# An earlier order of the first loads and 51 dummy products in a fused attention and FFN kernel

## The chip, the cores and the metric

The kernel runs on one core of one Trainium2 chip. The metric is the device time of one execution in microseconds, the median of several. A core has five engines that run side by side and meet only at semaphores: TensorE (PE) multiplies matrices, VectorE (DVE) and ScalarE (ACT) read its results and compute row by row, GpSimd (POOL) does small work in on-chip memory and issues some transfers, and SyncE (SP) issues the other transfers. Transfers are carried out by 16 DMA engines, which all queues share.

## The reference

For each of 8 batches with 12 heads, 448 positions and 64 values a head, the reference computes attention whose scores are mixed over the heads before the softmax and after it, and then a feed-forward network on all 3584 positions:

```python
scores = scale * np.matmul(q, k.transpose(0, 1, 3, 2))
scores = np.einsum('bhij,hg->bgij', scores, w_pre)
scores = scores - np.max(scores, axis=-1, keepdims=True)
attn = np.exp(scores)
attn = attn / (np.sum(attn, axis=-1, keepdims=True) + 1e-09)
attn = np.einsum('bhij,hg->bgij', attn, w_post)
attn_out = np.matmul(attn, v)
x = attn_out.transpose(0, 2, 1, 3).reshape(B * S, H * D)   # 3584 x 768
h = np.maximum(x @ w_in, 0.0)                              # 3584 x 2048
out = h * h @ w_out                                        # 3584 x 768
```

Inputs and output are float32; the kernel computes its products in bf16 with float32 sums.

## The kernel before, in words

**Stages of a batch.** q, k and v are loaded from HBM and cast to bf16 on the way, by transfers that POOL issues (`load_q`, `load_tail`, `load_kv`, lines 318 to 333). In the first two batches TensorE turns q and k with transposes (`t_qk` and `t_tail`, line 491 and line 519), and VectorE or ScalarE copies the results back. `score` (line 629) multiplies them: one product of 448 columns gives the scores of 128 positions of a head, which are cast from PSUM into `snat`. The scores must then be laid out anew, with positions and heads together along the partitions, so that the mixing over heads becomes a product: a transfer within on-chip memory that SP issues does this (`relayout`, `move`, line 658). In the following these transfers are called relayouts. Each of 45 chunks of a batch holds ten positions with their twelve heads. In the first 18 chunks of batch 0 a relayout of 315 KB serves three chunks, each mixed by three products (line 749, `wtri_all` with tiles lent by `osb` and `h2`); all other chunks have a relayout of their own of 105 KB and one product (line 753).

`chunk` carries a chunk through: the mixing product on TensorE; the row minimum on VectorE (line 758; signs are turned, so it stands for the maximum); the exponential with its row sum on ScalarE (line 761); the reciprocal on VectorE (line 767); the scaling of the second mixing matrix by it on GpSimd (line 770); four products that mix and transpose back (line 777); and a copy out of PSUM by VectorE or ScalarE (lines 395 and 397). When the chunks of a part are through, `av` multiplies by v (line 817). The FFN follows in units of 128 or 256 positions (`unit`): products with w_in (line 870), relu on ScalarE (line 883), the square on GpSimd (line 886), products with w_out (line 902), a copy on VectorE, and stores that SP issues. Units of FFN work have the lowest priority, so they fill TensorE's gaps; the first unit can begin only when the first parts of batch 0's attention are through.

**What sets the order.** All this work is first described as operations with an engine, a duration, a priority and dependencies. `Planner.run` plays it through before the program is built: at each moment each engine takes the ready operation with the lowest priority number, PSUM banks are given out, and two queues, LOAD and DMA, stand for the transfers. The order that comes out is the order in which each engine's instructions are written down. On the chip an engine keeps to that order, whatever arrives first. A chunk's priority is its number; its relayout has the number less `AHEAD` (line 43), which is the lead, in chunks, by which scores and relayouts go in front.

**The first batch.** Three transfers for k, two for the tails of q and three for q come first (`LOADS0`). The operation `started` stands for POOL's set-up and these eight issues. `first_batch` (line 1022) then waits for `opened`, a tiny copy on POOL of the first scores into `hold` (line 1036): only after it are v's two halves issued (`load_half`), and after them the six tiles of w_in (`load_w1`, line 988), each of 128 rows, 512 KB in bf16. The loads for batch 1 and the four parts of w_out (`load_w2`) follow at set chunks. `LAST_W1` (line 77) has no use in this version.

Of the kernel before, what the change touches and what calls it, by code (L numbers as in the profile page):

```python
# [39 lines left out]
PIECE = NPAIR // 2  # L40
NE = 6
NSCH = 11
AHEAD = 7.4
FIFO = 50
ROWS, COLS = 1, 2
TURN = 95
STAY = 2
# [26 lines left out]
TRI_IN = (0, 1)  # L74
W2_AT = [18, 21, 24, 27]
Q1_AT = [13, 16]
LAST_W1 = 4
TAIL0, Q0 = 19, 0.7
EARLY0 = 0

# [17 lines left out]
        self.last, self.wait = -1, -1  # L98


class Planner:

    def __init__(self):
        self.ops = []
        self.banks, self.most = [], {}

    def add(self, eng, ns, pri, fn, deps=(), lat=60, bank=None, frees=None, mode=0):
# [9 lines left out]
    def run(self):  # L119
# [22 lines left out]
        t, mode = 0, 0  # L142
        queues = {"LOAD": Queue(), "DMA": Queue()}

        def settle():
# [13 lines left out]
        while True:  # L159
            for eng, heap in ready.items():  # L160
                if eng in queues:
                    x = queues[eng]
                    y = queues["LOAD"]
                    if eng == "DMA" and x.op is None and heap and y.op is not None and x.last != t and x.wait < t:
                        ahead = max(0.0, y.left - (t - y.at) * y.rate) + sum(z[2].rows[0] for z in ready["LOAD"])
                        x.wait = t + int(min(ahead, FIFO) * y.op.rows[1])
                        heapq.heappush(events, (x.wait, n, None))
                        n += 1
                    if eng == "DMA" and x.wait > t:
                        continue  # L170
                    while x.op is None and heap:
                        op = heapq.heappop(heap)[2]
                        op.eng, op.at = eng, t
                        order.append((op, []))
                        if op.rows[0] == 0:
                            heapq.heappush(events, (t + op.lat, n, op))
                            n += 1
                            continue
                        x.op, x.left, x.at, x.rate = op, float(op.rows[0]), t, 0.0
                        settle()  # L180
                    continue
                if busy[eng] > t:
                    continue
                kept, short, first = [], False, None
                while heap:
                    item = heapq.heappop(heap)
                    op = item[2]
                    if op.eng is not None:
                        continue
                    wide = len(op.bank) > 1  # L190
                    if not fits(op) or (short and op.bank and op.bank[0][0] in HOLD):
                        short = short or wide
                        kept.append(item)
                        continue
# [12 lines left out]
                    args = []  # L207
                    break
                else:
                    item = None  # L210
                    if first is not None:
                        kept.remove(first)
                        item, op, args = first, first[2], []
                if item is not None:
# [21 lines left out]
            while events and events[0][0] == t:  # L236
# [21 lines left out]
                for x in op.next:  # L258
# [4 lines left out]
                        n += 1  # L263
                    elif x.left == 0:
                        push(x)
        assert len(order) == len(self.ops)
        return order


# [1 line left out]
def kernel(  # L271
# [57 lines left out]
    def load_kv(dst, src, b, h0, h1):  # L329
# [654 lines left out]
    w1_in, later = [], {}  # L984
    w2_in = [add("W2", 0, 0, lambda: None, lat=0) for i in range(4)]

    def load_w1(c2, pri, more=()):
        w1_in.append(load(16, (152, 148), pri, lambda: nc.gpsimd.dma_start(
            out=w1[c2][:, :], in_=moe_w_in[c2 * 128:(c2 + 1) * 128, 0:DFF], max_dma_last_dim=4096,
        ), [started, *more]))  # L990

    def load_w2(f4, n):
        f_, c_ = 8 * (f4 % 2), 384 * (f4 // 2)
# [3 lines left out]
        ), gate(n))  # L997
        done.next.append(w2_in[f4])
        w2_in[f4].left += 1

    def load_half(b, n, x, deps):
        h0 = x * H // 2
        v_in[b].append(load(42, (46, 58), n, lambda: load_kv(vs, v, b, h0, h0 + H // 2), deps))
# [17 lines left out]

    def first_batch():
        for i in range(NPAIR):
            if i == 0:
                v_in[0] = []
                for x in range(0):
                    load_half(0, -30 + x, x, [started])
        for p in range(NPAIR):
            t_qk(0, p)
        for g in range(2):  # L1030
# [1 line left out]
        for r in (1, 0):  # L1032
            for p in groups(0, r):
                score(0, r, p)
        hold = sb.tile([P, NPAIR], BF16, name="hold")
        opened = add("POOL", 150, -6, lambda: nc.gpsimd.tensor_copy(
            out=hold[:, :], in_=store_of(0, 0)[:, 0:NPAIR, 0],
        ), scopy[0, 0])
        for x in range(0, 2):
            load_half(0, -5 + 0.1 * x, x, [opened])  # L1040
        for i in range(NPAIR):
            load_w1(i, -4 + 0.1 * i, [opened])
        for n, c in enumerate(ORDER0):
            if c in C0[2:]:
                for p in groups(0, block_of(c)[0]):
# [50 lines left out]
    for b in range(B):  # L1096
# [4 lines left out]
        if b + 1 < B:  # L1101
# [4 lines left out]
                )  # L1106
            load_v(b + 1, (b + 1) * NCHUNK + 6, av_op[b, 0] + av_op[b, 1])

    guard = tc.manual_schedule(engines={
        mybir.EngineType.PE, mybir.EngineType.DVE, mybir.EngineType.Activation, mybir.EngineType.Pool, mybir.EngineType.SP,  # L1110
    })
# [33 lines left out]
```

## Time and profile before

| | |
|---|---|
| time, median of 3 runs | 590.29 us (589.7 to 591.21) |
| the profiled execution, its own time | 591.14 us |
| its span, first to last instruction | 589.4 us |
| TensorE busy | 565.2 us, 96% of the span, 5751 products |
| VectorE busy | 486.1 us, 82% |
| ScalarE busy | 471.3 us, 80% |
| GpSimd busy | 326.2 us, 55% |
| mean granted clock of TensorE | 0.99 |
| w_in's six transfers, 512 KB each | 21.8 us from issue to landing, median |
| v's transfers, 336 KB each | 9.6 us, median over all batches |

How to read it: the page cuts the span into 40 slices of 14.7 us and gives one digit for each, in tenths. TensorE's products are pipelined and their ends are modelled, so a busy TensorE is not TensorE at its peak; a single product's duration holds a fixed share besides its columns. The row PEclk is the clock granted to TensorE; 1.00 also stands where the profile has no record of a change yet. The rows of single instructions give start, duration, engine, line, operation, result and operands, and in brackets how long the engine had been idle before it and what ended that. `SPq` and the issues on POOL are the instructions that start transfers; how long the transfer itself takes is seen from who waits for it. In the rows of the DMA queues, q0 holds what GpSimd issues, here the loads, and q1 what SP issues, here relayouts and stores. Shares of DMA time above 1 occur, since packets of both queues are in flight together; they mean that the engines are full.

### The profile page before, as it was taken

What the parts mean: (1) busy time and instruction counts of PE and PEld (TensorE: products, weight loads), DVE (VectorE), ACT (ScalarE), POOL (GpSimd) and SP (SyncE); (2) the same over time, 40 slices, a digit from 0 to 9 for tenths busy, and PEclk for the clock granted to TensorE, in tenths of its full rate; (3) what the DMA queues carried; (4) which work ended last, traced back from release to release, by engine and by line L of the source; (5) the groups of instructions that cost most, each with busy time, mean ns of one, the idle gap of its engine ahead of it and who ended that gap; (6) DMA issues with size and microseconds to landing.
All of it is one profiled execution on the core that took longest, in us unless ns stands there. A gap on an engine that the chain in (4) does not pass through costs nothing.

```text
span 589.4 us, 17018 instructions
## 1 busy us (share of the span) xinstructions
PE 565.2 (96%) x5751; PEld 403.8 (69%) x5751; DVE 486.1 (82%) x1240; ACT 471.3 (80%) x1239; POOL 326.2 (55%) x600
## 2 busy tenths in 40 slices
PE   5698999999999999999999999999999999999996
PEld 3346766776668766776867776876767866867783
DVE  4697999997798998999898898989798898989201
ACT  4597998888988988989898878888889988788330
POOL 4436647546667437744865538744865624735340
PEclk9897999999999999999999999999999999999999
DMA  8899969984596449964596639974497547322021
GB/s 95 181 217 215 211 135 166 181 168 130 104 203 147 131 127 164 187 152 135 102 187 168 144 90 169 183 142 140 89 175 186 136 107 144 105 83 78 2 53 55
DMA packets 132086, 82.33 MB, mean 140 GB/s; under 512 B 59582, under 2 KB 126286, under 8 KB 131998
## 3 DMA queue, kind: packets, MB, share of 16 engines
q1 hardware_dynamic: 85214, 58.42, 40.6%
q0 software_dynamic: 46784, 22.81, 30.6%
q8 instruction: 45, 0.74, 0.5%
q14 instruction: 43, 0.35, 0.2%
HBM read 45.62 MB, written 11.01 MB: 96 GB/s over the span
## 4 chain that ended last, share of the span: by engine, by line
PE 84%; ACT 5%; DMA 5%; issue 2%; DVE 1%; SPq 1%; POOL 1%; DVEq 0%; POOLq 0%; ACTq 0%
PE bank L902 24%; PE bank L870 24%; PE bank L777 12%; PE bank L753 10%; PE bank L817 7%; PE bank L629 6%; DMA sch<-snat 3%; ACT es L761 2%; DMA osb<-snat 1%; SPq L658 1%; ACT snat L397 1%; ACT hr L883 1%; DVE mn L758 1%; PE bank L491 1%; DMA qt<-in_q_dram 1%
## 5 line engine op out<-in xcount | busy, mean ns | idle before, releaser
L761 ACT ACTIVATE es<-bank,mn 120x448 bf16<-120x448 f32 x360 | 229.4, 643 | 40.2 <-DVE mn L758 35.1
L770 POOL TENSOR_SCALAR wq<-wback,rc 120x120 bf16<-120x120 f32 x360 | 130.5, 367 | 179.4 <-DVE rc L767 104.2
L758 DVE TENSOR_REDUCE mn<-bank 120x1 f32<-120x448 f32 x360 | 209.5, 609 | 8.4 <-PE bank L749 5.2
L902 PE MATMUL bank<-w,h 128*128 128x384 bf16 x896 | 174.3, 325 | 0.9 <-ACT es L761 0.5
L395 DVE CAST atb<-bank 112x480 bf16<-112x480 f32 (+3 forms) x227 | 142.1, 634 | 30.8 <-PE bank L777 27.8
L870 PE MATMUL bank<-xt,w 128*128 128x256 bf16 (+1 forms) x1632 | 164.5, 254 | 0.2
L870 PEld LDWEIGHTS <-w 128*128 128x128 bf16 x1632 | 135.7, 98 | 21.9 <-issue 2.3
L886 POOL TENSOR_TENSOR h<-hr 128x512 bf16<-128x512 f32 x112 | 116.2, 1039 | 54.7 <-ACT hr L883 52.2
L777 PEld LDWEIGHTS <-es 120*112 120x112 bf16 (+1 forms) x1440 | 116.9, 130 | 39.5 <-issue 8.1
L777 PE MATMUL bank<-wq,es 120*112 120x120 bf16 (+1 forms) x1440 | 129.6, 218 | 2.8 <-POOL wq L770 1.9
L902 PEld LDWEIGHTS <-h 128*128 128x128 bf16 x896 | 83.5, 97 | 55.1 <-issue 5.6
L753 PE MATMUL bank<-sch,wmix 120*128 120x448 bf16 x334 | 103.9, 355 | 1.3 <-DMA sch<-snat 0.9
L395 DVE CAST snat<-bank 128x448 bf16<-128x448 f32 x164 | 96.0, 612 | 6.3 <-PE bank L629 3.5
L397 ACT CAST atb<-bank 112x480 bf16<-112x480 f32 (+3 forms) x157 | 82.3, 540 | 15.7 <-PE bank L777 14.2
L883 ACT ACTIVATE hr<-bank 128x512 f32<-128x512 f32 x112 | 67.1, 599 | 31.0 <-PE bank L870 25.2
L397 ACT CAST snat<-bank 128x448 bf16<-128x448 f32 x172 | 84.9, 550 | 4.3 <-PE bank L629 3.2
L761 ACT ACTIVATION_READ_ACCUMULATOR es<-bank,mn 120x1 f32 x360 | 75.7, 210 | 0.0
L767 DVE RECIPROCAL rc<-sm 120x1 f32<-120x1 f32 x360 | 52.7, 153 | 14.4 <-ACT es L761 12.3
L917 DVE COPY osb<-bank 128x384 f32<-128x384 f32 x56 | 30.7, 549 | 31.6 <-PE bank L902 31.3
L753 PEld LDWEIGHTS <-wmix 120*128 120x128 bf16 x342 | 30.3, 98 | 19.0 <-issue 7.8
L629 PE MATMUL bank<-kt,qz 64*128 64x448 bf16 x288 | 42.6, 354 | 0.5 <-ACT atb L397 0.2
L817 PE MATMUL bank<-atb,vs 112*64 112x192 bf16 (+3 forms) x864 | 42.2, 255 | 0.5 <-ACT atb L397 0.5
(57 smaller groups left out, 248.6 us busy)
## 6 DMA issues: line engine op xcount, KB each, us to landing
sch<-snat SPq DMA_DIRECT2D x318, 105.0 KB
out_dram<-osb SPq DMA_DIRECT2D x23, 360.0 KB
vs<-in_v_dram POOLq DMA_DIRECT2D x16, 336.0 KB, 9.6
ks<-in_k_dram POOLq DMA_DIRECT2D x14, 336.0 KB, 10.0
qs<-in_q_dram POOLq DMA_DIRECT2D x14, 288.0 KB, 8.2
w<-in_moe_w_in_dram POOLq DMA_DIRECT2D x6, 512.0 KB, 21.8
w<-in_moe_w_out_dram POOLq DMA_DIRECT2D x4, 768.0 KB, 24.5
out_dram<-osb SPq DMA_DIRECT2D x8, 192.0 KB
```

The lines of the kernel that those rows point to most:

```text
L395: nc.vector.tensor_copy(out=out_, in_=in_)
L397: nc.scalar.copy(out=out_, in_=in_)
L629: nc.tensor.matmul(slot[:, 0:S], lhsT=lhsT, rhs=kt[i][half, :, at_, :], start=True, stop=True)
L753: nc.tensor.matmul(slot[:, 0:S], lhsT=wm[0:rows, :], rhs=src[0:rows, :], start=True, stop=True,)
L758: nc.vector.tensor_reduce(out=mn[i][0:rows, :], in_=slots[mk][0:rows, 0:S], axis=AX.X, op=ALU.min)
L761: nc.scalar.activation(out=es[i][0:rows, 0:S], in_=slots[mk][0:rows, 0:S], func=ACT.Exp, scale=-1.0, bias=mn[i][0:rows, 0:1], accum_out=sm ...
L770: nc.gpsimd.tensor_scalar(out=wq[i][0:rows, :, 0:ns], in0=wback[0:rows, :, 0:ns], scalar1=rc[i][0:rows, 0:1], scalar2=1.0, op0=ALU.mult, o ...
L777: nc.tensor.matmul(slot[0:P_KEYS, jb * H * ns:(jb + 1) * H * ns], lhsT=es[i][0:rows, jb * P_KEYS:(jb + 1) * P_KEYS], rhs=wq[i][0:rows, :, ...
L817: nc.tensor.matmul(v_[64 * hh:64 * hh + 64, i, 0:x1 - x0], lhsT=vs[:, 2 * c2 + hh, jb, :], rhs=atb[half][:, jb, 2 * c2 + hh, x0:x1], start ...
L870: nc.tensor.matmul(slot[:, j * w:(j + 1) * w], lhsT=w1[c2][:, (f0 + j) * 128:(f0 + j + 1) * 128], rhs=xt[:, c2, a:z], start=(c2 == 0), sto ...
L886: nc.gpsimd.tensor_tensor(out=h2_[:, f0:f0 + nf, 0:w], in0=hr[gi % 2][:, :].rearrange("p (f c) -> p f c", f=nf), in1=hr[gi % 2][:, :].rear ...
L902: nc.tensor.matmul(slot[:, 0:384], lhsT=h2_[:, ft, mt * 128:(mt + 1) * 128], rhs=w2[:, ft, nt * 384:(nt + 1) * 384], start=(ft == 0), stop ...
```

## The change

It has three parts. First, the copy into `hold` and the wait for it go. The loads of the first batch depend on `started` alone and follow the q loads: one tile of w_in, then v's two halves, then the other five tiles.

Second, the planner gets a model of TensorE's clock and puts dummy products where it has TensorE idle. `Clock` divides time into spells of 3413 ns and keeps how much of each TensorE worked; below a share of `DROP` the plan's clock falls to half, from `RISE` on it returns, and TensorE's operations last twice as long in between. Before 130 us, if TensorE has nothing to do and a bank is free, and the clock is low or the last spell was worked for less than 0.55, a dummy is written down: a product of a tile of zeros, `still`, 256 columns wide, into the next free bank, which nobody reads. There are 51: 18 at the very start, before k arrives; 17 between the last scores of the second block and the first chunk's product; 3 among the products of chunks 20 to 22; and 13 among the first chunks of batch 1, ahead of the last attention products of batch 0. `still` is zeroed on VectorE as its first instruction.

Third, `AHEAD` goes from 7.4 to 7.2.

```diff
-AHEAD = 7.4
+AHEAD = 7.2
+IDLE_NS, IDLE_COLS, IDLE_FROM, IDLE_END, IDLE_LOW = 112, 256, 1300, 130000, 0.55
+SPELL, PHASE, DROP, RISE = 3413, 1700, 0.4, 0.8
-LAST_W1 = 4
+LAST_W1 = 1
+class Clock:
+    def __init__(self):
+        self.slow, self.edge, self.spells = True, PHASE, []
+
+    def at(self, t):
+        while t >= self.edge:
+            share = self.share(self.edge - SPELL, self.edge)
+            self.slow = share < (RISE if self.slow else DROP)
+            self.edge += SPELL
+        return 2 if self.slow else 1
+
+    def share(self, a, b):
+        return sum(max(0, min(b, z) - max(a, y)) for y, z in self.spells[-400:]) / (b - a)
...
+                if item is None and eng == "PE" and free and IDLE_FROM <= t < IDLE_END and (
+                    clock.at(t) > 1 or clock.share(t - SPELL, t) < IDLE_LOW
+                ):
+                    op = Op({"PE": 0}, 0, 0, self.still, [], None, None, mode)
+                    op.eng, op.ns, op.at = "PE", IDLE_NS * clock.at(t), t
+                    clock.spells.append((t, t + op.ns))
+                    order.append((op, [free[0], mode]))
...
-                        op.ns += TURN * (op.mode != mode)
+                        op.ns = (op.ns + TURN * (op.mode != mode)) * clock.at(t)
+                        clock.spells.append((t, t + op.ns))
...
+    still = sb.tile([P, IDLE_COLS], BF16, name="still")
+    nc.vector.memset(still[:, :], 0.0)
...
         for i in range(NPAIR):
-            if i == 0:
-                v_in[0] = []
-                for x in range(0):
-                    load_half(0, -30 + x, x, [started])
+            if i == LAST_W1:
+                load_v(0, 0.1 + i, [started])
+            load_w1(i, 0.1 + i)
...
-        hold = sb.tile([P, NPAIR], BF16, name="hold")
-        opened = add("POOL", 150, -6, lambda: nc.gpsimd.tensor_copy(
-            out=hold[:, :], in_=store_of(0, 0)[:, 0:NPAIR, 0],
-        ), scopy[0, 0])
-        for x in range(0, 2):
-            load_half(0, -5 + 0.1 * x, x, [opened])
-        for i in range(NPAIR):
-            load_w1(i, -4 + 0.1 * i, [opened])
...
+    def stand(slot, mode):
+        k_, m_ = P // 2 if mode == ROWS else P, P // 2 if mode == COLS else P
+        nc.tensor.matmul(
+            slot[0:m_, 0:IDLE_COLS], lhsT=still[0:k_, 0:m_], rhs=still[0:k_, :], start=True, stop=True,
+        )
```

More of the change, by code (lines that the diff above doesn't have):

```diff
@@ L107, in __init__ @@
         self.banks, self.most = [], {}
+        self.still = None
     def add(self, eng, ns, pri, fn, deps=(), lat=60, bank=None, frees=None, mode=0):
@@ L140, in fits @@
             return len(free) >= size and room[kind] >= size and (room["mix"] >= size or kind == "f")
-        t, mode = 0, 0
+        t, mode, clock = 0, 0, Clock()
         queues = {"LOAD": Queue(), "DMA": Queue()}
@@ L213, in run @@
                         item, op, args = first, first[2], []
+                if item is None and eng == "PE" and free and IDLE_FROM <= t < IDLE_END and (
[5 more added lines that the diff above has]
+                    order.append((op, [free[0], mode]))
+                    busy[eng] = t + op.ns
+                    heapq.heappush(events, (t + op.ns, n, None))
+                    n += 1
                 if item is not None:
@@ L265, in run @@
                         push(x)
-        assert len(order) == len(self.ops)
+        assert len(order) >= len(self.ops)
         return order
@@ L985, with load_w1 @@
     w2_in = [add("W2", 0, 0, lambda: None, lat=0) for i in range(4)]
-    def load_w1(c2, pri, more=()):
+    def load_w1(c2, pri):
         w1_in.append(load(16, (152, 148), pri, lambda: nc.gpsimd.dma_start(
             out=w1[c2][:, :], in_=moe_w_in[c2 * 128:(c2 + 1) * 128, 0:DFF], max_dma_last_dim=4096,
-        ), [started, *more]))
+        ), [started]))
     def load_w2(f4, n):
@@ L999, in load_w2 @@
         w2_in[f4].left += 1
-    def load_half(b, n, x, deps):
-        h0 = x * H // 2
-        v_in[b].append(load(42, (46, 58), n, lambda: load_kv(vs, v, b, h0, h0 + H // 2), deps))
     def load_v(b, n, deps):
@@ L1107 @@
             load_v(b + 1, (b + 1) * NCHUNK + 6, av_op[b, 0] + av_op[b, 1])
+    add("FIRST", 0, 0, lambda: None, lat=IDLE_FROM)
+    def stand(slot, mode):
[3 more added lines that the diff above has]
+        )
+    pl.still = stand
     guard = tc.manual_schedule(engines={
```

## The prediction

> **What bounds the kernel now.** I read the page's slices first, then the time by stretches of the front, then the order of time on TensorE, SP and POOL, then the two DMA queues by stretches.
>
> ```profile
> PE   5698999999999999999999999999999999999996
> PEclk9897999999999999999999999999999999999999
> ```
>
> Past slice 6 TensorE is full at full clock to the end, and from 55 us on its waits sum to 2.9 us (1.2 for GpSimd's scalings, the rest in halves and less). Time lost before some 57 us is thus lost for good; a gain there is kept as long as TensorE stays fed. The change acts in that front. By stretches (TensorE, weight loads, VectorE, ScalarE, GpSimd, granted clock, DMA share, GB/s):
>
> ```profile
> 15.00:20.00 5.00, 2.81 (x28) 1.08 (x25) 3.61 (x10) 3.71 (x9) 4.49 (x7) 1.00 0.52 92
> 20.00:24.30 4.30, 1.43 (x8) 0.52 (x6) 1.99 (x5) 1.95 (x6) 2.31 (x5) 1.00 1.11 188
> 24.30:28.00 3.70, 3.67 (x15) 1.93 (x16) 2.01 (x4) 1.38 (x4) 0.36 (x1) 0.54 1.15 272
> 28.00:45.00 17.00, 15.65 (x113) 7.66 (x112) 16.79 (x42) 15.92 (x41) 5.51 (x13) 1.00 1.07 221
> 45.00:51.30 6.30, 4.06 (x26) 2.11 (x24) 6.30 (x18) 5.21 (x14) 6.01 (x12) 0.77 1.27 208
> 51.30:57.00 5.70, 5.67 (x114) 4.97 (x115) 2.34 (x8) 3.58 (x13) 2.00 (x4) 0.66 1.40 220
> ```
>
> From 28 to 51.3 us VectorE (and nearly ScalarE) is the bound: a wait of another engine costs nothing there. VectorE's holes lie at 15 to 28 and at 51.3 to 57 us, and the granted clock is down in both. Who makes the first hole (SP issues the relayouts; x9 are three chunk products):
>
> ```profile
> 15.15 1.82 SPq L658 DMA_DIRECT2D osb<-snat  x2
> 19.56 1.86 PE L749 MATMUL bank<-osb,wtri_all 120*128 120x448 bf16 x9 [2.15 <-DMA osb<-snat]
> 24.33 2.31 PE L749 MATMUL bank<-osb,wtri_all 120*128 120x448 bf16 x6 [2.91 <-DMA osb<-snat]
> ```
>
> The first relayout lands 4.4 us after its issue, the second 8.3 us. Why, the DMA queues tell (q0 carries the loads, q1 the relayouts: packets, MB, share), for 12 to 18, 18 to 24, 24 to 31 and 31 to 39 us:
>
> ```profile
> q1 hardware_dynamic: 102, 0.27, 19.1%
> q0 software_dynamic: 31, 0.01, 1.7%
> ...
> q0 software_dynamic: 987, 0.51, 73.7%
> q1 hardware_dynamic: 196, 0.41, 23.0%
> ...
> q0 software_dynamic: 673, 0.76, 62.4%
> q1 hardware_dynamic: 503, 1.09, 51.5%
> ...
> q0 software_dynamic: 777, 1.50, 99.4%
> q1 hardware_dynamic: 169, 0.29, 11.4%
> ```
>
> The loads stand still for six microseconds (12 to 18). Then v, in many small packets, pushes the relayouts to 0.41/6 = 0.07 MB/us; beside w_in they get 1.09/7 = 0.16; alone they had 0.19 (in the second from 17). w_in alone gets 1.50/8 = 0.19.
>
> **The loads' new order.** The hold copy goes (POOL, 0.19 us). Eight issues (six of w_in at 0.72 us, two of v at 0.80, together 5.9) move from 15.7 to 8.4 us on POOL, which waits 6.9 us there (the hold's idle row). They end by 14.4, ahead of POOL's first softmax scaling at 22.35, so nobody waits for POOL. They pass nothing on SP. In q0 they follow the q loads, which drain by 11.7. The first w_in tile (0.51 MB at 0.19) runs to 14.4. v (0.69 MB, at 0.63/4 = 0.16 as k and q had from 8 to 12 us) has 0.37 MB through by 16.7, when the first relayout's packets start; the other 0.32, at v's shared 0.51/6 = 0.085, last to 20.5. Relayout 1 (0.32 MB) gets 0.26 by then and the rest at 0.16: it lands at 20.9 instead of 19.56. Relayout 2 then has w_in beside it instead of v: 0.32/0.16 = 2.0, so 23.0 instead of 24.33.
>
> (a) Chunk 3's products begin 1.3 us earlier. At full clock three products take 0.62 instead of the 1.15 of the row at 24.33, so VectorE, 0.77 behind the product's start as now for chunk 0 (19.56 to 20.33), has chunk 3 at about 23.8 instead of 25.56: -1.8. The first three chunks come 1.3 later, into a hole, and end before 23.8. TensorE then works through from 20.9, so the clock drop at 24.48 may not come: nine products at 558 ns instead of 353 are 1.85 of TensorE, inside VectorE's hole of 1.69. I count 0.3 of that, since the idle ahead of 20.9 may still pull the clock down. Sum -2.1; ends -3.5 (the hole of 24.3 to 28 gone too) and +2.0 (rival S).
>
> (b) w_in ends some 5 us earlier than the 47.4 of its last tile (issued 20.8, landing 26.6 later): q0 has used the idle six. TensorE's waits for relayouts at 45 to 51.3 us (about 2.9 with those of its weight loads) shrink, but VectorE is 6.30 of 6.30 busy over them, which is the cover. Batch 1's q and k, behind w_in in q0, land earlier also. -0.3; ends -2.9 (VectorE's order gives way too) and 0.3 (schedule against it).
>
> **The dummies.** One has 256 columns; at full clock twelve such products take 1.31 us, 109 ns each. Cold ones cost double: a chunk product takes 558 against 353, and the 205 more are its 448 columns at 0.43 ns (109/256) once again.
>
> (c) The first 18 last 18 x 0.218 = 3.9 us. The new memset on VectorE (0.13 to 0.38; the row of 384 words took 0.38) stands ahead of it: 1.2 to 5.1 us, inside TensorE's wait of 5.4 us for k. Their effect:
>
> ```profile
> L491 PE MATMUL bank<-ident,qs x12: 313/314/316, 12.7 to 13.2; 128*64 128x128 bf16 x12
> L491 PE MATMUL bank<-ident,qs x12: 219/219/243, 14.3 to 14.6; 128*64 128x128 bf16 x12
> ```
>
> TensorE was cold until some 14.2 us though the profile calls it 1.00, and the chain of waits from 7.75 to 14.7 is TensorE throughout. Warm, the streaming halves, but VectorE and ScalarE are 4.06 and 3.66 of 5 busy from 10 to 15 us, and relayout 1 waits for their casts: at most 0.9 earlier. Half of that: -0.4; ends -0.9, 0.
>
> A rule speaks against this part. The Trainium skill (TensorE: Matmul & The Clock Gate, Part 4: PE-mode transpose) says that transposes do not count as TensorE work the way products do, so full clock does not engage for them. The trace agrees so far: TensorE was busy without a gap from 8 us, mostly with transposes, and still cold six microseconds later. By that rule the warmth of the dummies is lost again before the scores.
>
> (d) 17 dummies (1.9 us) stand before the first chunk product, where TensorE idles 2.15 us now and 3.5 by (a): 0. Three stand near the products of chunks 20 and 21 (0.33, under VectorE's bound). Thirteen stand among batch 1's first products and the last attention products of batch 0 (1.42), where TensorE now has holes of 0.62, 0.60 and 0.47 (86 to 90 us). A dummy also waits for the last reader of the bank that the plan took for free, but the next product of that bank would wait for the same. Hidden: 0; the sixteen all on the path: 1.8. I take +0.5, nearer to the hidden end, since the holes of 1.69 lie where the thirteen stand.
>
> (e) The clock falls at 48.37 and 24.48 and rises at 27.89 and 55.19, all apart by multiples of 3.41 us. The second spell stretches 48 attention products to 2.77 us; the same 48 take 1.53 at 72.92. With the products around them it costs up to 2.0 of VectorE's 3.36 idle. The clock's steps may fall elsewhere in the next execution, since 3.41 us is their spacing and the profile of one execution gives one phase. Three dummies ahead and fewer waits for relayouts keep the clock up in perhaps two of five runs: -0.8; ends -2.0, 0.
>
> (f) Lead 7.2 instead of 7.4, with dummies and loads in the plan, reorders the engines from chunk 6 on; SP's first 57 instructions keep their order. No stage shows a price; bounds are TensorE's 3 us of waits past 55 us, either way. I take 0, and half of it for the range.
>
> Sum: -2.1 - 0.3 - 0.4 + 0.5 - 0.8 = -3.1 against the profiled execution (591.14, of it 589.4 span; the 1.7 around it stay). Its median of runs is 590.29, 0.85 lower, so 587.2.
>
> **Rivals.**
> - T, warmth lost: the rule above, (c) gives 0: 587.6. For it: cold until 14.2. Against: of the 6.6 us from 7.75 on, 2.95 are scores (0.56, 0.55, 0.93 and 0.91 by the rows), which do count.
> - N, front gain not kept: relayout 1's +1.3 cancels 2's -1.3, and both spells come back. VectorE's bound from 28 us covers the rest: -0.3 - 0.4 + 0.5 = -0.2, 590.1. For it: three dummies are few against 6.8 us of spell.
> - S, slower: relayout 1 meets w_in and v in full flow and flies 8.3 us like relayout 2 does now, landing at 23.45. The 1.99 us of VectorE from 20 to 24.3 move behind that, the spells stay: +2.0 - 0.3 + 0.5 = +2.2, 592.5. It decides from a landing of some 22.5 on. For it: v's 0.07 MB/us. Against: by 16.7 half of v should be through.
> - G: all good ends, -3.5 - 0.3 - 0.9 + 0.5 - 2.0 = -6.2: 584.1.
>
> **How the numbers follow.** This forecast 0.28, T 0.20, N 0.25, S 0.17, G 0.10. 0.3% is 1.8 us, about what a measurement here tells from no change: faster is below 588.5, slower above 592.1. With (f)'s 1.5 around each case: faster 0.24 + 0.16 + 0.10 + 0.03 = 0.53; slower 0.16 + 0.08 = 0.24; the rest 0.23. The range takes G's end and S with a little: 584.2 to 593.0; the forecast's own is 585.7 to 588.7.
>
> **What would show it.** The first chunk product's wait for its relayout ending at 20 to 21.5 us, and the next at 22.5 to 23.5, almost without idle between; a granted clock of 1.00 from 24.3 to 28; q0 moving from 12 to 18 us; w_in's last tile down by 43; transposes at 219 ns before 14 us (T: at 300 or more). Wrong if the first product comes after 22.5 (S), or the clock is 0.5 twice again (N).

## The result, and the profile after

The changed kernel takes 594.81 us (median of 6 runs, 593.39 to 597.26), the kernel before 590.79 (6 runs, 589.7 to 592.12): a ratio of 1.007, with a 95% interval of 1.0046 to 1.0094. It is some 4 us slower. The forecast was 587.2, and its range ended at 593.0. The profiled execution took 593.39, with a span of 591.6.

The slices of the changed kernel, TensorE and its granted clock:

```profile
PE   7787999999999999989999999999999999999996
PEclk8798999999999999999999999999999999999999
```

TensorE is as full as before past the front, but for a digit of 8 in the 18th slice (250 to 265 us), where before had a 9. By the same stretches as before (TensorE, weight loads, VectorE, ScalarE, GpSimd, granted clock, DMA share, GB/s):

```profile
15.00:20.00 5.00, 3.02 (x25) 1.81 (x22) 2.57 (x7) 2.68 (x7) 0.00 (x0) 0.98 1.28 210
20.00:24.30 4.30, 2.39 (x7) 0.99 (x7) 0.62 (x1) 0.42 (x1) 0.00 (x0) 0.50 1.10 272
24.30:28.00 3.70, 3.70 (x21) 1.82 (x19) 2.79 (x8) 2.51 (x9) 1.07 (x3) 0.69 1.10 274
28.00:45.00 17.00, 14.71 (x109) 7.24 (x108) 16.91 (x40) 15.46 (x39) 5.66 (x14) 1.00 0.59 134
45.00:51.30 6.30, 4.41 (x35) 2.48 (x34) 6.30 (x18) 6.23 (x20) 5.79 (x11) 1.00 1.19 155
51.30:57.00 5.70, 4.56 (x102) 3.81 (x102) 3.24 (x10) 3.21 (x11) 2.34 (x5) 0.73 1.35 231
```

From 20 to 24.3 us VectorE works 0.62 us, before it was 1.99; from 24.3 to 28 it works 2.79 instead of 2.01. VectorE's hole now lies earlier and has not shrunk, and both cold spells are there again: the clock is at 0.50 from 19.8 to 26.6 us, twice as long as in the kernel before (24.5 to 27.9), and from 53.9 to 57.3, half as long (48.4 to 55.2). The order of time in the front (start, duration, what; `L780` is the first chunks' product, `L689` the issue of a relayout, `L1131` the dummies), first of PE and then of SP:

```profile
1.06 4.02 PE L1131 MATMUL bank<-still 128*128 128x256 bf16 x18 [1.06 <-DVE still L365]
...
16.04 2.03 PE L1131 MATMUL bank<-still 64*128 64x256 bf16 x17
21.91 2.40 PE L780 MATMUL bank<-osb,wtri_all 120*128 120x448 bf16 x6 [3.85 <-DMA osb<-snat]
```

```profile
14.12 2.12 SPq L689 DMA_DIRECT2D osb<-snat  x2
```

Relayout 1 is issued 1.03 us earlier than before and lands 2.35 us later, at 21.9: a flight of 7.8 us, from the issue to the first product, where it was 4.4. The products behind it run at half clock, so that the next chunks follow 1.12 us apart. VectorE starts on the row minimum of chunk 3 one microsecond later than before (first line before, second line changed):

```profile
25.56 0.62 DVE L758 TENSOR_REDUCE mn<-bank 120x1 f32<-120x448 f32 x1 [3.04 <-PE bank L749]
```

```profile
26.58 0.62 DVE L789 TENSOR_REDUCE mn<-bank 120x1 f32<-120x448 f32 x1 [0.37 <-PE bank L780]
```

Why the flight is longer, the queues tell. From 14 to 18 us the loads' queue q0 has the first of these lines and q1 has none; in the microsecond from 18 to 19 the first packets of relayouts appear (second line); 18 to 24 us are the last two. The first share is above 100% with next to nothing in another queue, so packets of a single queue overlap too:

```profile
q0 software_dynamic: 1368, 0.76, 138.4%
...
q1 hardware_dynamic: 17, 0.05, 12.8%
...
q0 software_dynamic: 446, 0.81, 73.3%
q1 hardware_dynamic: 321, 0.76, 36.1%
```

At 18 us, 3.9 us after its issue, relayout 1 had not moved a byte, while the loads moved 0.76 MB from 14 us on; its first packets come between 18.5 and 19, so 4.4 to 4.9 us after the issue. Then both queues share, 0.13 MB/us each, and TensorE goes from relayout 1 to relayout 2 without a wait. In the kernel before, the first packets came 1.4 to 1.9 us after the issue (15.15, and 28 packets from 16.5 to 17).

### The profile page after: what moved, and what is told of

The parts are those of the page before. It is cut to its first block, busy times and chain, and to the rows that moved or that the text cites. A ratio compares the mean times of both kernels' runs of the same rounds, so it can differ in the third digit from the quotient of the medians.

```text
span 591.6 us, 17109 instructions
## 1 busy us (share of the span) xinstructions
PE 568.5 (96%) x5802; PEld 406.3 (69%) x5802; DVE 485.9 (82%) x1241; ACT 472.6 (80%) x1240; POOL 325.1 (55%) x598
## 4 chain that ended last, share of the span: by engine, by line
PE 81%; DMA 8%; DVE 6%; issue 2%; ACT 2%; SPq 1%; POOL 0%; DVEq 0%; POOLq 0%; ACTq 0%
PE bank L933 24%; PE bank L901 22%; PE bank L808 12%; PE bank L784 10%; PE bank L848 6%; PE bank L660 6%; DMA sch<-snat 4%; DVE mn L789 2%; DMA kt<-kn 2%; DVE atb L426 1%; DMA osb<-snat 1%; DVE snat L426 1%; PE bank L780 1%; ACT es L792 1%; DMA qt<-in_q_dram 1%
## 5 line engine op out<-in xcount | busy, mean ns | idle before, releaser
L426 DVE CAST atb<-bank 112x480 bf16<-112x480 f32 (+3 forms) x233 | 144.1, 631 | 31.1 <-PE bank L808 29.5
L808 PEld LDWEIGHTS <-es 120*112 120x112 bf16 (+1 forms) x1440 | 112.7, 130 | 38.7 <-issue 10.5
L808 PE MATMUL bank<-wq,es 120*112 120x120 bf16 (+1 forms) x1440 | 124.9, 217 | 5.5 <-POOL wq L801 4.6
L784 PE MATMUL bank<-sch,wmix 120*128 120x448 bf16 x334 | 102.7, 353 | 2.7 <-DMA sch<-snat 2.1
L428 ACT CAST atb<-bank 112x480 bf16<-112x480 f32 (+3 forms) x151 | 79.7, 540 | 13.6 <-PE bank L808 12.4
```

Of the source, the lines that this page charges most:

```text
L426: nc.vector.tensor_copy(out=out_, in_=in_)
L428: nc.scalar.copy(out=out_, in_=in_)
L784: nc.tensor.matmul(slot[:, 0:S], lhsT=wm[0:rows, :], rhs=src[0:rows, :], start=True, stop=True,)
L808: nc.tensor.matmul(slot[0:P_KEYS, jb * H * ns:(jb + 1) * H * ns], lhsT=es[i][0:rows, jb * P_KEYS:(jb + 1) * P_KEYS], rhs=wq[i][0:rows, :, ...
```

## The experiments

Each ratio below is against runs of the kernel before on the same chip, with its 95% interval. The new parts are called by three names: the order (lead and plan), the early loads, and the dummies. Where the order of the kernel before is kept, loads and dummies were moved or added in the finished order, so nothing else changes place. Two kernels were measured twice, and each pair came out 0.0017 or so apart, 1 us; differences of that size are at the edge of what can be told.

**The order, without early loads, with and without the dummies.** `e1_gated` keeps the changed kernel's order and its 51 dummies, but lets v and w_in wait for the hold copy again; `e6_order` is the same without the dummies.

```diff
+order = [x for x in order if x[0].fn is not stand]      # e6_order only
+at = 1 + max(i for i, x in enumerate(rest) if any(x[0] is y for y in scopy[0, 0]))
+order = rest[:at] + [(opened, [])] + [(x, []) for x in first_] + rest[at:]   # v0 v1 w0 .. w5
```

> The changed kernel with its order on every engine kept, dummies and lead 7.2 too; only the eight first loads go back behind the hold copy, in the old sequence (v's halves, then six tiles of w_in). Theory L (the early v loads hold relayout 1 back, and that is the loss): relayout 1 lands about 18.5 us instead of 21.9, the clock drop at 19.8 goes, and the time is 589 to 591.5, like the kernel before. Theory O (the new order past the front, from the lead and the new plan, is the loss): relayout 1 is early all the same, but the time stays at 593 to 595. Theory D (the 51 dummies stand in the way): 592 to 594.

> The changed kernel's order on every engine with the first loads back behind the hold copy and no dummies at all: the kernel before in all but the order. Theory O: 594.5 to 596 (2 above the same with its 51 dummies, since the front ones are worth about 2). If the order costs nothing: 591 to 592.

Measured: `e1_gated` 593.56 us, 1.0034 (1.0011 to 1.0057); `e6_order` 594.28 us, 1.006 (1.0028 to 1.0092). Both are near what theory O had, and relayout 1 lands at 18.3 in `e1_gated`, as forecast. The order alone costs 0.6%, 3.5 us, nearly as much as the whole change, and without its dummies the changed order is not shorter, which speaks against theory D. Where it loses, the stretches from 84 to 90 us and 84 to 132 us tell. The kernel before:

```profile
84.00:90.00 6.00, 4.27 (x58) 3.05 (x57) 5.51 (x16) 5.97 (x17) 3.47 (x7) 1.00 0.46 116
84.00:132.00 48.00, 46.27 (x520) 32.62 (x518) 45.24 (x118) 41.41 (x114) 28.23 (x56) 1.00 0.90 166
```

`e6_order`, the changed order alone:

```profile
84.00:90.00 6.00, 3.31 (x26) 2.17 (x24) 6.00 (x17) 4.55 (x14) 2.48 (x6) 0.83 0.53 149
84.00:132.00 48.00, 44.49 (x470) 30.80 (x469) 43.54 (x113) 38.49 (x106) 27.74 (x56) 0.93 0.85 160
```

Here batch 0 ends and batch 1 begins. In the plan before, VectorE and ScalarE share this work almost evenly (5.51 and 5.97 of 6); in the new one VectorE is full and ScalarE has 1.45 us free, and TensorE behind them loses 0.96 us. The chain there runs through GpSimd: TensorE waits for the scaling of the second mixing matrix, and GpSimd for a reciprocal that stands in VectorE's full order (`e6_order`):

```profile
85.88 0.37 PE L809 MATMUL bank<-wq,es 120*112 120x120 bf16 x4 [1.65 <-POOL wq L802]
```

```profile
87.74 0.37 POOL L802 TENSOR_SCALAR wq<-wback,rc 120x120 bf16<-120x120 f32 x1 [1.32 <-DVE rc L799]
```

In the kernel before the longest such wait of TensorE from 84 to 90 us is 0.62. In `e6_order` the clock also drops (0.93 over 48 us is 6.8 us at half speed). Over these 48 us TensorE makes 470 products instead of 520. The changed kernel itself:

```profile
84.00:90.00 6.00, 4.20 (x48) 3.18 (x46) 6.00 (x17) 4.73 (x14) 2.82 (x7) 1.00 0.59 167
84.00:132.00 48.00, 45.52 (x514) 31.72 (x512) 45.06 (x117) 40.31 (x111) 28.39 (x58) 1.00 0.87 171
```

The same full VectorE, but the clock stays up. Seven of the 22 more products from 84 to 90 us are dummies, and `e1_gated`, which has them too, also stays at 1.00. A second place is common to all kernels of this order, at 254 to 257 us, where before TensorE had no idle at all from 250 to 300 us. The chain of waits of the changed kernel, and TensorE's waits there:

```profile
246.61 9.12 DMA kt<-kn
```

```profile
PE bank L660 <- DVE atb L426: 0.9, 1, 0.9
PE bank L660 <- DMA kt<-kn: 0.7, 1, 0.7
```

VectorE's copies of the next k (`kn`) stand in its order ahead of copies that TensorE needs, and wait 1.85 us for the transfer that still reads the old `kn`. TensorE idles 1.62 us from 250 to 300 us in the changed kernel, 1.40 in `e1_gated`, 1.96 in `e6_order`.

**Is it the shorter lead, or any new plan?** `e4_lead`, `e15_lead73` and `e16_lead76` are the kernel before with only its lead changed to 7.2, 7.3 and 7.6 and planned anew. `e9_lead74` is the changed kernel, planned with a lead of 7.4.

```diff
-AHEAD = 7.4
+AHEAD = 7.2      # e4_lead; 7.3 in e15_lead73, 7.6 in e16_lead76
```

> The kernel before with the lead 7.2 instead of 7.4 and nothing else, so that the planner orders the work anew. Theory O: 592 to 595, and a stall past 60 us that the kernel before lacks. Theories L and D: 590 to 591.5.

> The changed kernel with the lead back at 7.4; the planner orders everything anew (55 dummies, early loads). If the lead 7.2 is what makes the order bad: 590.5 to 592.5. If any new plan costs about as much as this one (the order is a draw, the lead only one of the dice): anything from 588 to 600, and the stage where it falls behind is another one than in the changed kernel (there 84 to 120 and 252 to 264 us).

> The kernel before with only its lead set to 7.3 and the work planned anew; loads and wait for the hold copy as before, no dummies. Theory R (the plan before is one good draw among many, and any other plan costs some microseconds, whatever the lead): 593 to 599 us, ratio 1.004 to 1.014. Theory A (a shorter lead is what costs, some 10 us for 0.2 by the run with 7.2 alone): half of it, 594 to 597, so this run alone tells little; it is the pair with 7.6 that decides.

> The kernel before with only its lead set to 7.6 and planned anew. Theory R (any other plan costs): 593 to 599 us, ratio 1.004 to 1.014, like 7.3. Theory A (shorter is worse, longer better): at most as long as before, 583 to 591.5, ratio below 1.001.

Measured: lead 7.2 600.19 us, 1.0169 (1.0122 to 1.0217); 7.3 597.47 us, 1.0103 (1.0076 to 1.013); 7.6 599.54 us, 1.0139 (1.011 to 1.0168); the changed kernel at 7.4 597.28 us, 1.0101 (1.0076 to 1.0125). `e9_lead74`'s profile is of an execution of 727.71 us with the clock at 0.75, so where that plan falls behind isn't known. A longer lead costs as much as a shorter one, and the old lead does not save the new plan. At the same lead of 7.2, `e4_lead` costs 10 us (more than any theory had for it) and `e6_order` 3.5. So the length of the lead doesn't set the price: the five other plans tried for this work are all behind the one of the kernel before: by 3.5 us (`e6_order`), by 6 to 10 (the three leads), and by 6 with the new loads and dummies (`e9_lead74`). Why the plan of the kernel before is the best of the six isn't shown; if its lead was picked from several by their times, that alone would put it ahead of plans that weren't. In two of the lead runs the loss begins at the same place. `e15_lead73`, then `e16_lead76`, 84 to 90 us:

```profile
84.00:90.00 6.00, 3.32 (x28) 1.75 (x25) 5.97 (x17) 4.95 (x14) 2.63 (x6) 1.00 0.34 86
```

```profile
84.00:90.00 6.00, 3.27 (x27) 1.73 (x24) 6.00 (x17) 4.60 (x13) 2.59 (x6) 1.00 0.34 83
```

`e15_lead73` and `e4_lead` each add a stall of their own, where VectorE waits in its order for a transfer (1.8 and 3.6 us) and TensorE for VectorE. In `e16_lead76` TensorE's longest sum is for GpSimd's scalings. Of TensorE's waits in `e15_lead73`, 84 to 132 us, in `e4_lead`, 420 to 500 us, and in `e16_lead76`, from 60 us on:

```profile
PE bank L753 <- DVE snat L395: 2.0, 1, 2.0
```

```profile
PE bank L777 <- DVE snat L395: 2.3, 1, 2.3
```

```profile
PE bank L777 <- POOL wq L770: 5.6, 11, 1.5
```

**The loads.** `e2_loads` is the kernel before with only the loads moved as in the change. `e7_v_last`, `e10_w_then_v` and `e11_w0_early` keep the order before and carry the 35 front dummies of `e3_dummies` (below), with other loads: all early and v last; all behind the hold copy and v last; only the first tile of w_in early.

```diff
+front = [named[x] for x in 'w0 v0 v1 w1 w2 w3 w4 w5'.split()]   # e2_loads, right after started, no hold copy
+front = [named[x] for x in 'w0 w1 w2 w3 w4 w5 v0 v1'.split()]   # e7_v_last, right after started, no hold copy
+rest[at:at] = w0 w1 w2 w3 w4 w5 v0 v1                           # e10_w_then_v, behind the hold copy
+rest[at:at] = w0                                                # e11_w0_early, right after started, the others behind the hold copy
```

> The kernel before with its order on every engine kept and no dummies; only the eight first loads move to right behind the q loads, as w_in tile 0, v's halves, w_in tiles 1 to 5, and the hold copy goes. Theory L: relayout 1 is issued at 15.2 as before but lands at 21.5 to 22.5 instead of 19.56, and the time is 592.5 to 594.5. Theory O or D: 589.5 to 591.5 whatever relayout 1 does.

> The kernel before with its order, 35 front dummies, and the eight first loads right behind the q loads, but with all six tiles of w_in first and v's halves last. Theory V (v's small packets hold relayout 1 back, w_in does not): relayout 1 lands at 16.5 to 18.5 us and the time is 587 to 589.5, at or below the kernel with dummies alone. Theory Q (any load in full flow ahead of relayout 1 holds it back): relayout 1 lands at 20.5 to 22.5 and the time is 590.5 to 592.

> The kernel before with its order, 35 front dummies, the loads behind the hold copy as before, but w_in's six tiles ahead of v's halves. If v's small packets are what slows relayout 2 (0.07 MB/us beside v, 0.16 beside w_in): relayout 2 lands at 20.5 to 21.5 us instead of 23.3 and the time is 586.5 to 588.5, below the 589.5 with dummies alone. If not: 589 to 591.

> The kernel before with its order, 35 front dummies, one tile of w_in right behind the q loads and everything else behind the hold copy. If a queue of loads in full flow holds back relayout 1's first packets, one tile that drains by 14.6 us does not: relayout 1 lands by 18.6 and the time is 588.5 to 590. If one tile is enough to hold it back: it lands at 20 or later, and the time is 590.5 to 592.

Measured: `e2_loads` 592.21 us, 1.0019 (1.0001 to 1.0038); `e7_v_last` 591.44 us, 0.9999 (0.9974 to 1.0024); `e10_w_then_v` 592.56 us, 1.0022 (1.0005 to 1.004); `e11_w0_early` 591.01 us, 1.0002 (0.998 to 1.0025). The first chunk product in `e2_loads`, `e7_v_last` and `e1_gated`, where relayout 1 is issued at 14.07, 14.15 and 14.14:

```profile
22.28 4.58 PE L750 MATMUL bank<-osb,wtri_all 120*128 120x448 bf16 x15 [5.96 <-DMA osb<-snat]
```

```profile
22.32 4.92 PE L752 MATMUL bank<-osb,wtri_all 120*128 120x448 bf16 x14 [4.22 <-DMA osb<-snat]
```

```profile
18.33 1.86 PE L781 MATMUL bank<-osb,wtri_all 120*128 120x448 bf16 x9 [0.24 <-DMA osb<-snat]
22.94 2.42 PE L781 MATMUL bank<-osb,wtri_all 120*128 120x448 bf16 x6 [2.75 <-DMA osb<-snat]
```

With the loads in flow the flight is 8.2 us, whether v or w_in is what flows at that moment; with the queue empty it is 4.2. In `e7_v_last` q1 has a single packet up to 19 us, nearly five after the issue (first line, 18 to 19 us). In `e11_w0_early` the one tile has drained, the first packets come within 2 us of the issue at 15.00 (second line, 16 to 17 us), and the product starts at 19.38.

```profile
q1 hardware_dynamic: 1, 0.00, 0.8%
```

```profile
q1 hardware_dynamic: 44, 0.12, 40.6%
```

`e2_loads` and `e7_v_last` landed as theories L and Q had it; the time of `e2_loads` lies between its two forecasts. `e11_w0_early` landed between its two, with the time of the worse one. So what delays the relayout is a load in full flow at its issue, not v's small packets. These were not the brake of relayout 2 either: with v last and all behind the copy (`e10_w_then_v`) its products come at 24.09, not earlier, and the time was longer than either forecast; what that order costs isn't traced further.

```profile
18.22 1.86 PE L752 MATMUL bank<-osb,wtri_all 120*128 120x448 bf16 x9 [0.16 <-DMA osb<-snat]
24.09 2.42 PE L752 MATMUL bank<-osb,wtri_all 120*128 120x448 bf16 x6 [4.01 <-DMA osb<-snat]
```

What the late landing costs shows in pairs of profiles whose relayout 1 went out at the same time. VectorE starts on chunk 3 at 26.58 in the changed kernel and 24.28 in `e1_gated` (issues 14.12 and 14.14), at 26.44 in `e2_loads` and 24.08 in `e4_lead` (14.07 and 14.10), at 26.89 in `e7_v_last` and 24.64 in `e3_dummies` (14.15 and 14.30): 2.3 us each time. Where the one early tile has drained there is no price: 24.90 in `e11_w0_early`, 24.86 in `e13_35` (15.00 and 15.05).

The times agree, though each is hardly clear of its error: +1.1 us (`e2_loads` against before) and +2.1 (the changed kernel's 1.007 against `e1_gated`'s 1.0034). `e7_v_last` is 1.1 to 2.1 us above the 35 dummies alone, but it also has v last, and `e10_w_then_v`, with v last and no early loads, is 2.4 to 3.4 us above them. `e11_w0_early`, with its relayout in time, is no faster than `e7_v_last` (1.0002 and 0.9999), so the times alone would not have shown this.

**The dummies.** `e3_dummies` and `e13_35` are one kernel: the order and loads before, with 18 dummies at the start and 17 ahead of the first chunk's product. `e8_gap17` has only the 17. `e12_late13` and `e14_48` are again one kernel: the 35 and 13 late ones among batch 1's first chunks. `e5_no_late` is the changed kernel without its last 16.

```diff
+order = [dummy(banks[0], 0) for i in range(18)] + order                     # not in e8_gap17
+order[at:at] = [dummy(order[at][1][0], ROWS) for i in range(17)]            # ahead of the first chunk's product
+for n_, k_ in [(46, 6), (48, 1), (49, 6)]:                                  # e12_late13, e14_48
+    order[at:at] = [dummy(order[at][1][0], 0) for i in range(k_)]
+still_ = still_[35:]; order = [x for x in order if x not in still_]         # e5_no_late, in the changed kernel
```

> The kernel before with its order and its loads kept, and 35 dummies put in: 18 at the very start and 17 ahead of the first chunk's product. Theory D: 592 to 594. Theories L and O: relayout 1 issued about 1 us earlier (14.1) and landing by 18.6, time 589 to 590.8.

> The kernel before with its order and loads and only the 17 dummies ahead of the first chunk's product. If these carry the gain of the 35: 589 to 590, and no clock drop before 21 us. If the 18 at the start carry it: 591 to 592, relayout 1 issued between 14.1 and 15.2 as the clock's phase has it.

> The changed kernel with its order and early loads, without its last 16 dummies (the three by chunk 20 and the thirteen among batch 1's first chunks). Theory D2 (the late dummies stand in TensorE's way): 593 to 594, 0.8 to 1.7 below the changed kernel. Theory O (the order past the front is what costs): 594.5 to 595.5, the late dummies are hidden.

> The kernel before with its order and loads, the 35 front dummies and 13 more among batch 1's first chunk products, as in the changed kernel. If these keep the clock up at 88 to 96 us (where it fell in three of the profiles without them): 588 to 589.5 with no drop there. If they only stand in the way: 590 to 591.

> The order and loads of the kernel before, with 18 dummies at the start and 17 ahead of the first chunk's product, again and beside the next one on the same chip. If these 35 are a gain (as measured first, 0.9964): 588 to 589.5 us, ratio 0.994 to 0.998. If they are nothing (as the two runs that had them with something else, 0.9998 and 1.0002, would have it): 590 to 591.5, ratio 0.998 to 1.002, and then the 2 us between the kernels with and without dummies in the changed order are for the most part something else.

> The same with 13 more dummies ahead of the products of chunks 46, 48 and 49. If the 13 cost (1.4 us of TensorE by their number and the duration of one), this run is 1 to 2 us longer than the one with 35 on the same chip. If they lie in holes, both come out within 0.5 us.

Measured: 35 dummies 589.48 us, 0.9964 (0.9942 to 0.9986) the first time and 590.94, 0.9981 (0.996 to 1.0001) the second; 17 alone 590.29, 0.9975 (0.9953 to 0.9996); 48 dummies 590.96, 0.9998 (0.9978 to 1.0017), and beside the 35 on one chip 591.02, 0.9982 (0.9963 to 1.0001); the changed kernel without the last 16 597.23, 1.0093 (1.006 to 1.0127). The dummies are worth something between nothing and 2 us, and 1.5 in the changed order (`e6_order` to `e1_gated`), at the edge of what can be told. The 13 late ones cost nothing measurable: 35 and 48 agree to 0.1 us on one chip. `e12_late13` had no drop at 88 to 96 us and yet the time of the other case. `e5_no_late` missed both its forecasts: without its last 16 dummies the changed kernel is 1.4 us longer, not shorter, though within the error. That is all that the 51 are worth there, so the late ones may carry it. The profile shows what they prevent where TensorE starves. From 90 to 96 us, `e5_no_late`, then the changed kernel:

```profile
90.00:96.00 6.00, 4.56 (x69) 3.94 (x69) 3.60 (x12) 4.05 (x13) 3.51 (x8) 0.75 0.36 122
```

```profile
90.00:96.00 6.00, 5.80 (x86) 4.00 (x86) 4.88 (x13) 5.76 (x18) 3.77 (x8) 1.00 0.38 104
```

The 18 at the start warm TensorE in nine of eleven profiles, and not for long. Transposes of the changed kernel by start and duration (L522):

```profile
9.07 0.58 PE L522 MATMUL bank<-ident,ks 112*64 112x112 bf16 x16
...
10.07 0.96 PE L522 MATMUL bank<-ident,ks 112*64 112x112 bf16 x16
```

Sixteen transposes take 0.58 us at 9.07 and 0.96 again at 10.07; full clock returns at some 13 us, and the same falling back is in all nine, between 7.6 and 9.6 us. The Trainium skill (TensorE: Matmul & The Clock Gate, Part 4: PE-mode transpose) says that transposes do not count as work for the clock as products do. The fall agrees with that, but does not prove it: TensorE also idled 1.44 and 0.24 us in the 3.4 us ahead of it. The rises speak against it, and the measurement decides: in the kernel before the clock rises at 14.24 us, after 3.41 us in which TensorE was busy throughout, 1.81 us of it with transposes, and in the changed kernel at 12.96, after 3.37 us with 1.91 of transposes.

In `e12_late13` and `e9_lead74` the 18 do not warm it at all; the transposes behind them are cold (`e12_late13`):

```profile
5.61 0.96 PE L494 MATMUL bank<-ident,ks 112*64 112x112 bf16 x16 [0.52 <-DMA ks<-in_k_dram]
```

The clock's steps tell why. They lie on a grid of 3.41 us, with another phase in each execution. In the nine, TensorE was busy for 3.13 us or more of the 3.41 us that ended with the rise; in the other two, for 2.23 to 2.74 us of each of the two spells over which the dummies fell. In the kernel before, 3.08 us from 7.41 to 10.83 were not enough. The 18 last 4.0 us, so where an edge falls among them they fill neither spell. And where they do warm TensorE, nothing comes of it: relayout 1 goes out at 13.98 to 15.11 us with them and at 14.07 to 15.15 without, wherever the clock's later rise happens to lie.

**The sum.** Order +3.5 us, dummies -1.5, early loads +2.1: +4.1, against 4.1 measured (0.7% of 590.8). That it closes proves nothing: the three are the steps from the kernel before over `e6_order` and `e1_gated` to the changed kernel, and such steps always add up. By the other route, loads 1.1 (`e2_loads`) and dummies -1.1 to -2.1 (the 35, in the order before), the sum with the order's 3.5 would be 2.5 to 3.5. That the order is the largest of the three holds either way.

The profiles can be compared from start to end if one counts the columns that TensorE's products have streamed up to a time (dummies not counted, transposes and products over 64 rows half) and asks when the kernel before has streamed as many. The changed kernel is 0.6 us behind the one before at 60 us, 2.2 behind at 132, 0.4 at 250, and some 2.4 from 264 us to the end. `e6_order` goes from 1.3 us ahead at 60 to 2.9 behind at 132, is 2.3 behind at 252 and 4.8 at 264. The place at 60 us means little by itself: `e3_dummies` and `e13_35`, one kernel twice, are 1.3 us ahead and 0.5 behind there. Relayout 1 went out at 14.30 in the one and at 15.05 in the other, because TensorE's clock rose earlier or later (12 transposes around 12.5 us take 0.62 in the one and 0.85 in the other). The steps further back are the order's: from 60 to 132 us `e6_order` falls back by 4.2, and these two do not move by more than 0.2; from 252 to 264 us it falls back by 2.5, these two by 0.1 at most.

No version beats both kernels by much. The order and loads before with the front dummies (35, or the 17 alone) are the best found, 0.2 to 0.4% faster than the kernel before in three measurements, of which one does not exclude that there is no difference.

## Why the prediction was wrong

- **(f), the reorder, taken as 0, measured +3.5 us.** This is the step that failed most. "No stage shows a price" was read as a price of nothing. The bounds came from the waits of the kernel before past 55 us, but a new plan makes waits that the old trace cannot hold: VectorE full beside a ScalarE with time to spare at 84 to 90 us, and the stall at 254 us. The measured price is at the end of the bounds of 3 or beyond (1.7 to 5.4 by its interval), where half of them was used for the range, and the other plans go up to 10. In the prediction the order was a side effect of the change, and no case and no rival had a price for it; by the runs it is the larger part of the change. That a new order costs is measured; that VectorE's place in it is the reason is read from the traces, and no run changed that alone.
- **(a), relayout 1, forecast -2.1, measured +1 to +2.** The share of the bandwidth was nearly right (0.13 MB/us each, 0.16 assumed); the start was not. The step let the packets start at 16.7 as before, with loads in flow beside them. The issue came a microsecond earlier, by the clock's phase, and yet they started after 18.5. The step took its time from issue to first packet from a moment when the queue was empty. So relayout 1 landed at 21.9 instead of 20.9. Most of the rest is the clock, which the step put at 0.3: TensorE idled 3.85 us ahead of the landing, the clock was down from 19.8 on, and three products took 1.12 us instead of the 0.62 assumed. Chunk 3 reached VectorE at 26.58, where the forecast had 23.8. The trace of before shows the other case, and it was there to be read: at 38.60 and 39.42 SP issues two relayouts (the second line of five) beside w_in in full flow, and from 38.5 to 42.5 us q0 moves without q1 having a row at all.

```profile
38.60 0.76 SPq L658 DMA_DIRECT2D schl<-snat  x1
39.42 4.09 SPq L658 DMA_DIRECT2D sch<-snat  x5
```

```profile
q0 software_dynamic: 410, 0.79, 104.9%
q14 instruction: 1, 0.01, 0.5%
```

- **Rival S** had the right cause, the relayout that meets the loads, and nearly the right flight (8.3 forecast, 7.8 measured), but set its deciding point, a landing at 22.5, too late; 21.9 was enough, since the clock fell too. It lacked the order, and so came to 592.5. **Rival N**'s sign came, the clock at 0.5 twice, but not its reason: it had relayout 2's gain cancel relayout 1's delay. The chance of a slower kernel, 0.24, doesn't follow from the cases: with 1.5 us around each, S and N give about half of it.
- **(b)** w_in's last tile is down at 37.6 (43 forecast), and nothing came of it. Its 47.4 for the kernel before was a misreading: 26.6 us is the median of the last two tiles, and the last alone took 27.8, to 48.6. TensorE's idle from 45 to 51.3 us is 1.9 instead of 2.2, VectorE is 6.30 of 6.30 in both: the cover held.
- **(c)** The warmth was lost again at 9.5 us, as rival T said, but T's rule isn't needed for it: TensorE was busy for only 1.74 of the 3.41 us before. Nor was TensorE busy "without a gap from 8 us" for the clock in the kernel before: the spell that ended at 10.83 had a gap of 0.34, and the next, without one, ended in the rise. the sign named against T (219 ns before 14 us) was badly chosen, since it appears at 13.3, when the clock had risen a second time.
- **(d)** +0.5 for the late dummies is 0 by `e14_48`, and they help where the order starves TensorE. **(e)** In this profile the second spell is one step of 3.4 us long instead of two, but the first is two instead of one, so nothing is won; how often over many executions isn't known. (c), (d) and (e) together, -0.7, are inside the measured 0 to -2, but that is luck: of the three terms none came as it was reasoned.

## What to carry to other kernels

When an edit makes a planner or a scheduler run again, cost the new order as an edit of its own, and measure it alone: here six plans for the same work span 10 us, more than any of the deliberate parts. Idle time of a DMA queue is not free for the taking if a short transfer on another queue, with an engine waiting behind it, is issued into them; look in the old trace for the same transfer issued beside a load in flow, and take its time from there. Filling TensorE's idle with dummies cost nothing measurable here and kept the clock up where TensorE starved, but at the start it did nothing for the time; whether a burst warms TensorE depends on how it falls over the clock's 3.4 us spells.

## What was not expected of the hardware

- A transfer within on-chip memory that SP issues while loads issued by GpSimd are in full flow shows its first packet only 4 to 5 us later (4.4 to 4.9 in the changed kernel, 3.9 to 4.9 in `e7_v_last`, 3.9 to 4.4 at 38.6 us in the kernel before), and 1 to 2 us later when these are drained (`e11_w0_early`, before). Once started, both get about the same rate (0.81 and 0.76 MB from 18 to 24 us). The Trainium skill (DMA: Bandwidth & Descriptors, Queues, rings and completion order) says that each DMA engine goes round-robin between its queues, packet by packet. That agrees with the sharing after 18 us; by it alone relayout 1 should have begun to share soon after 14, where the trace has 1368 packets of q0 and none of q1. The measurement decides, but the place of the delay, ahead of the engines or in them, stays open: no run told them apart.
- The clock's falls and rises lie at multiples of 3.41 us from each other (24.48, 27.89, 48.37 and 55.19 in the kernel before) and at another phase in each execution. With them moves the first relayout: three kernels with the same front on TensorE have the rise at 11.80, 11.87 and 14.24 us, and the issue at 14.10 (`e4_lead`), 14.07 (`e2_loads`) and 15.15 (before). A microsecond between two single profiles of this front proves nothing.
